# Attention and gated FFN on one core: the last group's reload of gate and input in two lots, and the third kept sum loaded later and added in one run

## Chip, core and metric

The kernel runs on one core of a Trainium2 chip. The metric is the device time of one execution in microseconds (us). One execution was also taken by the hardware profiler; its instructions, waits and transfers are the trace that the text reads.

## What is computed

The reference, cut to what matters (B is the feed-forward branch, A the attention branch):

```python
xn = layernorm(x)                                    # x: 1 x 2048 x 512, bf16
q  = (xn @ wq) as 32 heads of 128                    # keys and values come from a cache of 2048 rows
o  = softmax(q @ k_cache.T * 128**-0.5) @ v_cache    # per head
s  = concat(o) @ wo                                  # 4096 -> 512
h  = relu(xn @ W_gate) * (xn @ W_up)                 # 512 -> 1792
g  = silu(h @ W_down)
return x + s * g
```

## The kernel before

**Blocks and positions.** The attention is 128 blocks (32 heads by four quarters of 512 query rows). A block has eight positions, 0 to 7, one for each pair of 128 keys; the text writes (119, 2) for block 119, position 2. At a position TensorE computes two score tiles (line L1626) three positions ahead, ScalarE takes their exponential into `PT` (L1638), and TensorE multiplies the `PT` of the present position with the values (L1735, 16 products), into the accumulator `ps_acc`. At the end of a block VectorE takes the reciprocal of the sums (L1655) and writes the normalized block to `Onorm` (L1658), of which there are four buffers, used in turn: block b writes buffer b mod 4, and its L1655 waits until the transpose of block b-4 out of that buffer has landed. That transpose is a DMA from SP's queue (`OT_store<-Onorm`, L1663). The values of the next block may go into `ps_acc` once `Onorm` is written.

**Ring of score banks.** The PSUM tile `ps_r` is three slots of two banks. Each pair of score tiles takes the next slot in turn, and so does each side product; a slot is free again when ScalarE or VectorE has read it. TensorE's instructions run in order, so a score tile whose slot isn't free holds all that is behind it.

**Side work.** Eight groups of four heads. While a group runs, the output projection of the group before it is computed by a scheme with seven products in place of eight (as Strassen's), each product's result being added into up to two of four sums `s_acc[:, J, i, :]` (J = 0 to 3, i = 0 to 3). The work is placed by hand: `plan` holds TensorE's products by (block, position), `side` holds calls for the other engines. At a position the score tiles come first, then the items of `plan`, then those of `side`, then the products with the values. The order in which an engine's instructions are issued in the program is the order in which it runs them.

**The last group** is blocks 112 to 127 (`fb` = 112, `LB` = 124). It has, beside the products:

- `load_kept(a)` (L1433), two DMAs that load a kept sum (a = 4, 5, 6; the third is a = 6) from DRAM to the buffers `KR[a]`; `add_kept(a, i)` (L1442) adds its part i on GpSimd into two sums, for a = 6 into J = 1 and J = 3. a = 6 is loaded at (115, 3) and added at (118, 1), (118, 3), (121, 2) and (121, 4) for i = 1, 3, 0, 2.
- `reload_g` at (115, 5): on SP's queue four DMA transposes of the gate from DRAM to `gT` (L1146) and four of the input to `xT` (L1147), alternating, then one plain load of `gN` (L1148).
- `emit_base(0, i)` at (119, 2) to (119, 5): VectorE multiplies a sum by `gT` (L1587; it waits for all four transposes of the gate), GpSimd adds `xT` (L1592; it waits for all four of the input).
- `prep_x(6, 5, part)` (L1488): GpSimd's operand sums for the product j = 5, at (120, 5) and (121, 1); `prep_x(6, 3, part)` for j = 3 at (122, 5) and (123, 1).
- `emit_one(2, 6, 4, 1, 0)` in `plan` at (121, 4): two products (L1457) in one ring slot, whose results VectorE adds (L1388) into J = 1 and J = 3 together, first for i = 1, then for i = 3. Each of the two additions waits for whatever last wrote the sums that it adds to.

On SP's queue the order from block 115 on is: `KT_sb` transpose for head 30 (L366), the reload, the values of head 30 (`V_sb`, L371), the transposes out of `Onorm` of blocks 115, 116, 117 and 118, the keys of head 31, its values, the transpose of block 119, and so on.

Of the kernel before, what the change touches and what calls it, by code (L numbers as in the profile page):

```python
# [30 lines left out]
def _wait(eng, tok):  # L31
    if tok is None:
        return
    sem, val = tok
    if val <= 0:
        return
    eng.wait_ge(sem.h, val)


def _wait_all(eng, toks):  # L40
    best = {}
    for t in toks:
        if t is None:
            continue
        sem, val = t
        k = id(sem)
        if k not in best or best[k][1] < val:
            best[k] = (sem, val)
    for sem, val in best.values():
        _wait(eng, (sem, val))  # L50


def bass_recurrent_scan__mha_block_cached__glu_gated_reglu__prompt_kernel(
# [20 lines left out]
    NT = S // 128  # L74
    DC = D // 128
# [33 lines left out]
    out_t = out2.rearrange("(n p) d -> p n d", p=128)  # L109
# [4 lines left out]
    sp = nc.sync  # L114
    pool = nc.gpsimd

    with ExitStack() as es:
# [9 lines left out]
        def newsem(unit=1):  # L127
            _cnt[0] += 1
            return _Sem(es.enter_context(nc.semaphore(f"sem{_cnt[0]}")), unit)
# [23 lines left out]
        def at_(off, shape, dt, name):  # L153
            _cnt[0] += 1
            return nc.alloc_sbuf_tensor_at(f"{name}_{_cnt[0]}", shape, dt, offset=base[0] + off)
# [68 lines left out]
        gN = at_(104448, [128, 4, D], BF16, "gN")  # L224
# [51 lines left out]
        sem_gn = newsem(16)  # L276
# [597 lines left out]
        def blk_of(gp):  # L874
            b, p = divmod(gp, NP)
            h, Q = divmod(b, QB)
            return b, h, Q, p
# [261 lines left out]
            for Q in range(QB):  # L1139
                sem_gs.sig(sp.dma_start(out_t[:, 4 * Q:4 * Q + 4, :], g_sb[:, 4 * Q:4 * Q + 4, :]))  # L1140

        def reload_g():
            _wait_all(sp, [u_tok["last"], u_tok["add"], sem_gs.cur()])
            for c in range(DC):
                cs = slice(c * 128, (c + 1) * 128)
                sem_gr.sig(sp.dma_start_transpose(gT[:, c, :], out2[:, cs]))  # L1146
                sem_xr.sig(sp.dma_start_transpose(xT[:, c, :], x2[:, cs]))  # L1147
            sem_gn.sig(sp.dma_start(gN[:], out_t[:, NT - 4:NT, :]))  # L1148

        def gu_h(Q, k, gate, up, waits):  # L1150
            _wait_all(pool, waits)
# [259 lines left out]
        one_to = {1: (0, 1), 7: (1, 2), 4: (1, 3)}  # L1411
# [21 lines left out]
                os_tok[("l", a)] = sem_rr[a].sig(sp.dma_start(  # L1433
                    K[n][:].rearrange("p i q -> p (i q)"), swap[a][:, 2 * n * NQ:2 * (n + 1) * NQ]))

        def add_kept(a, i):
            K = KR[a]
            _wait(pool, os_tok[("l", a)])
            for J in one_to[{4: 1, 5: 7, 6: 4}[a]]:
                _wait(pool, os_tok[(J, i)])  # L1440
                d = s_acc[:, J, i, :]
                os_tok[(J, i)] = sem_fo.sig(pool.tensor_tensor(d, d, K[i // 2][:, i % 2, :], ALU.add))  # L1442
# [424 lines left out]
        LB = NBLK - QB  # L1867
        side = {}
# [11 lines left out]
        for g in range(NG - 1):  # L1880
            b0 = (g + 1) * GB
            half = g < NG - 2
# [53 lines left out]
            for k, (j, (r, p)) in enumerate(zip((2, 6, 5, 3), px)):  # L1936
                side.setdefault((b0 + r, p), []).append((prep_x, g, j, 0))
                r, p = max((r, p), (xs[(2, 6, 5)[k - 1]] + 1, 1)) if k else (r, p)
# [28 lines left out]
        for b in range(NBLK):  # L1967
            pr, r = (b - 2) // 8 + 1, (b - 2) % 8
# [13 lines left out]
            elif 0 < pr < NPR:  # L1982
                c, step = r // 4, r % 4
# [9 lines left out]
        for n, (g, j, b) in enumerate(unit_at):  # L1993
# [14 lines left out]
            if j in (5, 7):  # L2008
                side.setdefault((b + 2, 0) if b + 1 in x_at else (b + 1, second[1]), []).append((add_unit, g, j))
        side.setdefault((GB + 1, 0), []).append((spill_g,))  # L2010
        side.setdefault((LB - 9, 5), []).append((reload_g,))
        for g in range(2, NG):
            b = GB * (g - 1)
            side.setdefault((b + 2, 0) if g == 2 else (b + 1, 4), []).append((load_unit_w, g, 0))
            side.setdefault((b + 2, 6) if g == 2 else (b + 2, 3), []).append((scale_unit_w, g, 0))
            b, p = (21, 6) if g == 2 else (b + 3, 5)
            side.setdefault((b, p), []).append((load_unit_w, g, 1))
            b, p = (22, 4) if g == 2 else (b + 1, 3)
# [1 line left out]
            sw = (22, 4) if g == 2 else (GB * (g - 1) + 6, 3)  # L2020
            side.setdefault(sw, []).append((sum_unit_w, g))
        fb = GB * (NG - 1)
        for r, p, a in ((1, 4, 4), (3, 1, 5), (3, 3, 6)):
            side.setdefault((fb + r, p), []).append((load_kept, a))
        for r, p, a, i in ((2, 2, 4, 0), (2, 4, 4, 2), (3, 1, 4, 1), (3, 3, 4, 3), (4, 0, 5, 1), (4, 2, 5, 3), (4, 4, 5, 0),
                           (4, 6, 5, 2), (6, 1, 6, 1), (6, 3, 6, 3), (9, 2, 6, 0), (9, 4, 6, 2)):
            side.setdefault((fb + r, p), []).append((add_kept, a, i))
        for i in range(4):
            side.setdefault((fb + 7, 2 + i), []).append((emit_base, 0, i))
        for i, part, (r, p) in ((1, 0, (11, 1)), (1, 1, (11, 2)), (3, 0, (11, 2)), (3, 1, (11, 3)), (0, 0, (11, 2)), (0, 1, (11, 4)), (2, 0, (11, 4)), (2, 1, (11, 5))):  # L2030
            side.setdefault((fb + r, p), []).append((emit_finish, i, part))
        for k, (J, i) in enumerate(((3, 1), (3, 3), (1, 1), (1, 3))):
            b, p = ((0, 1), (0, 3), (0, 5), (1, 0))[k]
            side.setdefault((LB + b, p), []).append((emit_base, J, i))
            c = 2 * (J // 2) + i // 2
            b, p = ((LB, 6), (LB + 1, 1), (LB + 1, 3), (LB + 1, 5))[k]
            side.setdefault((b, p), []).append((turn_base, c))
        for k, (J, i) in enumerate(((2, 0), (2, 2), (2, 1), (2, 3), (1, 0), (1, 2), (3, 0), (3, 2))):
            b, p = ((1, 2), (1, 3), (1, 4), (2, 4), (2, 3), (2, 5), (3, 1), (3, 3))[k]
# [21 lines left out]
        for gp in range(LAG, TOTP):  # L2061
# [3 lines left out]
            b, h, Q, p = blk_of(gp)  # L2065
# [111 lines left out]
```

## Time and profile before

| | |
|---|---|
| runs of the kernel before | 1236.59, 1237.78, 1238.86 us; median 1237.78 us |
| the profiled execution | 1237.87 us, of which the span of the instructions is 1236.5 us |
| TensorE busy | 1229.6 us of the span |
| ScalarE, VectorE, GpSimd busy | 1042.5, 875.9, 872.8 us |
| granted TensorE clock | 0.999 |

Times inside the profile are counted from the start of the span. In a row of the timeline stand the start, the duration, the engine, the line, the operation, what is written and read with shapes, and how many instructions were merged; in brackets the engine's idle time before it and what ended that. PE is TensorE, PEld its weight loads, DVE VectorE, ACT ScalarE, POOL GpSimd, SPq SP's queue of DMA issues. A row of the waits gives engine, tile and line of the waiter, what it waited for, the total in us, the number of times and the longest.

### The profile page before, as it was taken

The numbers are of one execution on the slowest core, as the hardware profiler recorded it, in microseconds if no ns is written. First come the engines' busy times: TensorE is split into PE (matmuls) and PEld (weight loads), VectorE is DVE, ScalarE is ACT, GpSimd is POOL, SyncE is SP. The second block draws the span as 40 slices with busy tenths as digits, with TensorE's granted clock in tenths as the row PEclk, the third lists the DMA queues.
The fourth block names the chain that finished last, engine by engine and source line by source line (L and its number), as shares of the span: only waits on it lengthen the run. The fifth ranks groups of instructions, "written<-read, shape, count | busy, mean of one in ns | idle before, by whom it ended". The sixth has DMA issues, their size and how long they took to land.

```text
span 1236.5 us, 29347 instructions
## 1 busy us (share of the span) xinstructions
PE 1229.6 (99%) x11922; PEld 816.2 (66%) x11922; DVE 875.9 (71%) x1335; ACT 1042.5 (84%) x1110; POOL 872.8 (71%) x994
## 2 busy tenths in 40 slices
PE   9999999999999999999999999999999999999998
PEld 5466666776666666666666666666666666666665
DVE  7668787667676767677676767676776767575587
ACT  4457877668899998999999999999999999989994
POOL 3355876313767868977978777976888777668668
PEclk9999999999999999999999999999999999999999
DMA  9712331223223534464636664584545464349726
GB/s 276 158 31 37 77 80 24 52 48 97 53 50 54 139 96 120 116 171 101 169 74 151 141 163 87 150 174 102 149 120 132 114 167 95 86 103 183 138 36 141
DMA packets 286646, 137.70 MB, mean 111 GB/s; under 512 B 253872, under 2 KB 279728, under 8 KB 280496
## 3 DMA queue, kind: packets, MB, share of 16 engines
q1 hardware_dynamic: 285168, 135.04, 47.2%
q8 instruction: 95, 1.56, 0.6%
q10 hardware_dynamic: 1344, 0.79, 0.2%
q14 instruction: 39, 0.32, 0.1%
HBM read 63.18 MB, written 30.41 MB: 76 GB/s over the span
## 4 chain that ended last, share of the span: by engine, by line
PE 97%; ACT 2%; DVE 0%; DMA 0%; issue 0%
PE ps_acc L1735 37%; PE ps_r L1626 35%; PE ps_r L1060 5%; PE ps_r L1523 4%; PE ps_r L1177 3%; PE ps_r L1238 3%; ACT PT L1638 2%; PE ps_r L924 2%; PE ps_r L739 2%; PE ps_r L743 2%; PE ps_acc L842 1%; PE ps_r L1457 1%; PE ps_r L1767 1%; PE ps_r L1554 1%; PE ps_r L1555 1%; PE ps_r L1848 0%
## 5 line engine op out<-in xcount | busy, mean ns | idle before, releaser
L1638 ACT ACTIVATE PT<-ps_r 128x1024 bf16<-128x1024 f32 x1024 | 990.7, 1026 | 127.7 <-PE ps_r L1626 112.7
L1735 PEld LDWEIGHTS ps_acc<-V_sb,PT 128*128 128x128 bf16 x8192 | 544.4, 98 | 224.7 <-issue 29.9
L1735 PE MATMUL ps_acc<-V_sb,PT 128*128 128x129 bf16 x8192 | 629.1, 220 | 1.2 <-ACT PT L1638 1.2
L1626 PE MATMUL ps_r<-QT_sb,KT_sb 128*128 128x512 bf16 x2048 | 601.0, 379 | 0.4
L1065 DVE TENSOR_TENSOR UVR<-UVR,ps_r 128x512 f32<-128x512 f32 (+1 forms) x228 | 168.7, 755 | 79.0 <-PE ps_r L1060 76.6
L1626 PEld LDWEIGHTS ps_r<-QT_sb,KT_sb 128*128 128x128 bf16 x2048 | 163.8, 98 | 31.2 <-ACT PT L1638 1.5
L1388 DVE TENSOR_TENSOR s_acc<-s_acc,ps_r 128x1024 f32<-128x1024 f32 x97 | 117.8, 1219 | 30.6 <-PE ps_r L1555 16.9
L1404 DVE TENSOR_TENSOR s_acc<-s_acc,ps_r 128x512 f32<-128x512 f32 x170 | 113.4, 685 | 27.7 <-PE ps_r L1523 21.9
L1655 DVE RECIPROCAL rz_sb<-ps_acc 128x4 f32<-128x4 f32 x127 | 23.2, 182 | 100.7 <-PE ps_acc L1735 97.0
L1488 POOL TENSOR_TENSOR TI<-OT_store 128x512 f16<-128x512 bf16 (+1 forms) x48 | 54.7, 1161 | 53.9 <-issue 22.2
L1658 DVE TENSOR_TENSOR Onorm<-ps_acc,rz_sb 128x512 bf16<-128x512 f32 x127 | 87.8, 691 | 4.4
L1488 POOL TENSOR_TENSOR TI<-OX 128x512 f16<-128x512 f16 x38 | 43.1, 1155 | 64.4 <-issue 62.8
L1065 DVE TENSOR_TENSOR QT_sb<-UVR,ps_r 128x512 bf16<-128x512 f32 x72 | 49.5, 687 | 34.3 <-PE ps_r L1060 31.9
L1025 POOL TENSOR_TENSOR TI<-xn_sb 128x512 f16<-128x512 f16 x48 | 55.8, 1163 | 18.4 <-PE ps_r L1060 18.4
L1332 POOL TENSOR_TENSOR WX<-Wo_sb 128x512 f16<-128x512 bf16 x7 | 8.1, 1156 | 68.5 <-DVE dbuf L1247 39.0
L1025 POOL TENSOR_TENSOR TI<-xn_sb,TI 128x512 f16<-128x512 f16 x48 | 55.9, 1164 | 0.0
L1523 PE MATMUL ps_r<-TI,SI 128*128 128x512 f16 x129 | 48.9, 379 | 0.0
L1060 PE MATMUL ps_r<-TI,SI 128*128 128x512 f16 x126 | 47.9, 380 | 0.0
L1025 POOL TENSOR_TENSOR TI<-xnT 128x512 f16<-128x512 bf16 x36 | 41.6, 1156 | 4.5 <-PE ps_r L1060 4.5
L1153 POOL TENSOR_SCALAR gB<-gB 128x512 bf16<-128x512 bf16 x14 | 20.8, 1485 | 30.4 <-DVE gB L1183 30.4
L1025 POOL TENSOR_TENSOR TI<-xnT,TI 128x512 f16<-128x512 bf16 x36 | 41.6, 1155 | 0.0
L1133 POOL TENSOR_TENSOR QT_sb<-UVR,UVR 128x512 bf16<-128x512 f32 x24 | 29.8, 1272 | 6.7 <-DVE UVR L1065 6.7
(236 smaller groups left out, 1461.6 us busy)
## 6 DMA issues: line engine op xcount, KB each, us to landing
sums<-s_acc SPq DMA_DIRECT2D x25, 1024.0 KB, 4.4
s_acc<-sums SPq DMA_DIRECT2D x22, 1024.0 KB, 5.7
V_sb<-in_A_v_cache_dram SPq DMA_DIRECT2D x32, 512.0 KB, 4.6
Wq_sb<-in_A_wq_dram SPq DMA_DIRECT2D x16, 256.0 KB, 3.5
Wo_sb<-in_A_wo_dram SPq DMA_DIRECT2D x8, 512.0 KB, 4.2
KR<-sums SPq DMA_DIRECT2D x6, 512.0 KB, 4.8
out_dram<-g_sb SPq DMA_DIRECT2D x4, 512.0 KB, 4.5
OT_store<-Onorm SPq DMA_TRANSPOSE x127, 2.8
```

The costliest lines, as they stand in the source:

```text
L1025: return sem_ui.sig(pool.tensor_tensor(dst, x, y, o))
L1060: return sem_up.sig(pe.matmul(dst, lhs, rhs, start=start, stop=stop, skip_group_check=True))
L1065: dve.tensor_tensor(dst, x, ps, ALU.add))
L1177: ins = pe.matmul(ps_r[:, bank, :], L(i), R(i), start=(i == 0), stop=(i == HC - 1))
L1388: t = sem_opa.sig(dve.tensor_tensor(dst, dst, sb, op))
L1404: t = dve.tensor_tensor(dst, dst, sb, op)
L1488: return sem_oi.sig(pool.tensor_tensor(dst, x, y, o))
L1523: return sem_op.sig(pe.matmul(dst, lhs, rhs, start=start, stop=stop, skip_group_check=True))
L1626: ins = pe.matmul(ps_r[:, 2 * s + tt, :], KT_sb[h % 2][:, t * 128:(t + 1) * 128], QT_sb[qt_slot[(h, Q)]][:], start=True, stop=True)
L1638: act.activation(PT[pb][:], ps_r[:, 2 * s:2 * s + 2, :], ACTF.Exp, scale=scale / WSC)
L1658: dve.tensor_tensor(Onorm[ob][:], o_ap, rz_sb[:].to_broadcast([128, 4, Dh]), ALU.mult))
L1735: ins = pe.matmul(o_ap, PT[pb][:, tt, j * 128:(j + 1) * 128], V_sb[vb][:, t, 0:VW], start=(t == 0 and j % 2 == 0), stop=(t == KT - 1 and j ...
```

## The change

```diff
-        def reload_g():
+        def reload_g(half):
             _wait_all(sp, [u_tok["last"], u_tok["add"], sem_gs.cur()])
-            for c in range(DC):
+            for c in range(DC // 2 * half, DC // 2 * (half + 1)):
                 cs = slice(c * 128, (c + 1) * 128)
                 sem_gr.sig(sp.dma_start_transpose(gT[:, c, :], out2[:, cs]))
                 sem_xr.sig(sp.dma_start_transpose(xT[:, c, :], x2[:, cs]))
-            sem_gn.sig(sp.dma_start(gN[:], out_t[:, NT - 4:NT, :]))
+            if half:
+                sem_gn.sig(sp.dma_start(gN[:], out_t[:, NT - 4:NT, :]))
...
-        def add_kept(a, i):
+        def add_kept(a, i, js=None):
             K = KR[a]
             _wait(pool, os_tok[("l", a)])
-            for J in one_to[{4: 1, 5: 7, 6: 4}[a]]:
+            for J in js or one_to[{4: 1, 5: 7, 6: 4}[a]]:
                 _wait(pool, os_tok[(J, i)])
...
-        side.setdefault((LB - 9, 5), []).append((reload_g,))
+        side.setdefault((LB - 9, 5), []).append((reload_g, 0))
+        side.setdefault((LB - 7, 1), []).append((reload_g, 1))
...
-        for r, p, a in ((1, 4, 4), (3, 1, 5), (3, 3, 6)):
+        for r, p, a in ((1, 4, 4), (3, 1, 5), (7, 4, 6)):
             side.setdefault((fb + r, p), []).append((load_kept, a))
         for r, p, a, i in ((2, 2, 4, 0), (2, 4, 4, 2), (3, 1, 4, 1), (3, 3, 4, 3), (4, 0, 5, 1), (4, 2, 5, 3), (4, 4, 5, 0),
-                           (4, 6, 5, 2), (6, 1, 6, 1), (6, 3, 6, 3), (9, 2, 6, 0), (9, 4, 6, 2)):
+                           (4, 6, 5, 2)):
             side.setdefault((fb + r, p), []).append((add_kept, a, i))
+        for k in range(8):
+            side.setdefault((fb + 9, 2 + k // 2), []).append((add_kept, 6, k % 4, (1,) if k > 3 else (3,)))
```

In blocks and positions: the reload's first two pairs of transposes stay at (115, 5); the other two pairs and the load of `gN` go to (117, 1), which on SP's queue is behind the values of head 30 and the transposes out of `Onorm` of blocks 115 and 116, and ahead of that of block 117. The load of the third kept sum goes from (115, 3) to (119, 4), behind the transpose of block 118 and ahead of the keys of head 31. Its eight additions (four parts into two sums) all stand in block 121: into J = 3 for i = 0 and 1 at position 2, for i = 2 and 3 at position 3, then into J = 1 for i = 0 and 1 at position 4, for i = 2 and 3 at position 5. The products of `plan` at (121, 4) are issued between those at position 3 and those at position 4.

## Prediction

> **What bounds the kernel now.** I read the page first, then the waits by engine, then the timeline of blocks 115 to 122, where every edit lies. The page's engine line and its chain:
>
> ```profile
> PE 1229.6 (99%) x11922; PEld 816.2 (66%) x11922; DVE 875.9 (71%) x1335; ACT 1042.5 (84%) x1110; POOL 872.8 (71%) x994
> PE 97%; ACT 2%; DVE 0%; DMA 0%; issue 0%
> ```
>
> TensorE has work all through and 97% of the chain that ends last is its own. The change takes no matmul away, so it can gain only where TensorE stands still. TensorE's waits over the whole trace, then the stretches before, in and after the one wait in this region (span, then busy time by engine):
>
> ```profile
> PE ps_acc L1735 <- ACT PT L1638: 1.2, 1, 1.2
> ...
> 1085.00:1155.00 70.00, 70.00 (x735) 48.29 (x733) 44.27 (x57) 65.56 (x70) 52.90 (x51) 1.00 0.76 160
> 1155.30:1157.60 2.30, 1.13 (x5) 0.19 (x3) 0.98 (x3) 2.30 (x3) 1.21 (x2) 1.00 0.57 96
> 1157.60:1226.00 68.40, 68.36 (x684) 45.82 (x685) 55.14 (x75) 55.78 (x60) 49.79 (x45) 1.00 0.42 71
> ```
>
> There is one stall, between blocks 119 and 120, and beside it no idle time that could be won or that could swallow a new delay. The timeline shows its size. Last products of block 119 and first of block 120, then the same border between blocks 121 and 122:
>
> ```profile
> 1154.39 0.62 PE L1735 MATMUL ps_acc<-V_sb,PT 128*128 128x129 bf16 x8
> 1157.64 0.27 PE L1735 MATMUL ps_acc<-V_sb,PT 128*128 128x129 bf16 x2 [1.21 <-ACT PT L1638]
> ...
> 1172.49 0.62 PE L1735 MATMUL ps_acc<-V_sb,PT 128*128 128x129 bf16 x8
> 1174.28 0.84 PE L1735 MATMUL ps_acc<-V_sb,PT 128*128 128x129 bf16 x12
> ```
>
> In both, four score tiles and two side products lie between. From start to start it is 3.25 us at the first border and 1.79 us at the second, so the stall costs 1.46 us. The row names ScalarE, but what block 120 needs is block 119's normalization, and VectorE's rows say who held that:
>
> ```profile
> 1147.37 0.18 DVE L1655 RECIPROCAL rz_sb<-ps_acc 128x4 f32<-128x4 f32 x1 [4.73 <-PE ps_acc L1735]
> 1148.83 1.22 DVE L1388 TENSOR_TENSOR s_acc<-s_acc,ps_r 128x1024 f32<-128x1024 f32 x1 [0.55 <-PE ps_r L1457]
> 1149.96 4.41 DVE L1587 SCALAR_TENSOR_TENSOR s_acc<-s_acc,gT 128x512 f32<-128x512 f32 x4
> 1156.59 0.18 DVE L1655 RECIPROCAL rz_sb<-ps_acc 128x4 f32<-128x4 f32 x1 [2.21 <-DMA OT_store<-Onorm]
> 1156.80 0.69 DVE L1658 TENSOR_TENSOR Onorm<-ps_acc,rz_sb 128x512 bf16<-128x512 f32 x1
> ```
>
> VectorE waited 2.21 us for the transpose that empties the buffer of block 115. `Onorm` is written at 1157.49 and TensorE goes on at 1157.64. SP's queue shows why that transpose was late (the landing of each follows in the next fence):
>
> ```profile
> 1086.82 3.01 SPq L366 DMA_TRANSPOSE KT_sb<-in_A_k_cache_dram  x1
> ...
> 1120.16 6.67 SPq L366 DMA_TRANSPOSE KT_sb<-in_A_k_cache_dram  x1
> 1126.95 2.78 SPq L1146 DMA_TRANSPOSE gT<-out_dram  x1
> ...
> 1134.97 2.68 SPq L1147 DMA_TRANSPOSE xT<-in_A_x_dram  x1
> 1137.69 3.08 SPq L1146 DMA_TRANSPOSE gT<-out_dram  x1
> ...
> 1143.20 2.51 SPq L1146 DMA_TRANSPOSE gT<-out_dram  x1
> ...
> 1148.81 0.51 SPq L371 DMA_DIRECT2D V_sb<-in_A_v_cache_dram  x1
> 1149.36 5.24 SPq L1663 DMA_TRANSPOSE OT_store<-Onorm  x1
> 1154.64 3.88 SPq L1663 DMA_TRANSPOSE OT_store<-Onorm  x3
> ```
>
> The landings, from the view of DMA issues over a window around one issue each (the 1149.36 one; the last gate transpose; the later half of the third kept sum), and VectorE's row that wrote block 115's buffer:
>
> ```profile
> OT_store<-Onorm SPq DMA_TRANSPOSE x1, 7.1
> ...
> gT<-out_dram SPq DMA_TRANSPOSE x1, 5.2
> ...
> KR<-sums SPq DMA_DIRECT2D x1, 512.0 KB, 7.2
> ...
> 1123.90 0.69 DVE L1658 TENSOR_TENSOR Onorm<-ps_acc,rz_sb 128x512 bf16<-128x512 f32 x1
> ```
>
> Block 115 was normalized at 1124.6, but its transpose stood behind the whole reload: issued at 1149.36, blocked for 5.24 us at issue, landed 7.1 us after its start, at 1156.5.
>
> **The reload in two lots: −1.46 us.** In the changed order the transposes of blocks 115 and 116 stand behind four transposes, not eight. Four take 1126.95 to 1137.65 to issue; even with the block of 5.24 us and the 7.1 us to landing, block 115's buffer is empty by 1138.2 + 7.1 = 1145.3, 9 us ahead of when it is wanted (about 1154.9: the last products start at 1154.39, and in the row of 1147.37 and its like VectorE follows by 0.5). Block 116's buffer is wanted one block later. The values of head 30 come earlier too. So the old stall goes whole; bounds 1.21 (the idle time in TensorE's row) to 1.46, and I take the latter, which counts the loss and not only the part shown as idle.
>
> What is late next there is the last gate transpose, since `emit_base` in block 119 waits for all four. Before, it landed at 1143.20 + 5.2 = 1148.4, and VectorE wanted it at 1149.96. Now it has in front of it the values (0.51 us of issue) and two `Onorm` transposes (the first 1.3 us, a third of the row of 3.88, to 5.24 us; the second 1.3), but not the load of the third kept sum, which moves behind. That load is 1 MB that stood in front of the keys: their issue took 6.67 us behind it and 3.01 us without, so the first lot starts 3.7 us sooner. Net, the landing moves by 0.5 + 1.3 + 1.3 − 3.7 = −0.6 us to 0.5 + 5.2 + 1.3 − 3.7 = +3.3 us: 1147.8 to 1151.7. The queue before the first `Onorm` transpose is shorter than in the old trace (four transposes and the values, where it was eight, `gN` and the values), so I take the middle, about 1150, which is a wait of nearly nothing. The four multiplications then end near 1154.4 and the reciprocal is wanted at 1154.9. GpSimd's additions behind them are 5.71 us long and its next job, the operand sums for j = 5, starts 4.3 us after they end:
>
> ```profile
> 1150.79 5.71 POOL L1592 TENSOR_TENSOR s_acc<-s_acc,xT 128x512 f32<-128x512 f32 x4 [3.78 <-DVE s_acc L1587]
> 1160.81 2.27 POOL L1488 TENSOR_TENSOR TI<-OT_store 128x512 f16<-128x512 f16 x2 [4.30 <-issue]
> ```
>
> so the input's landing may slip by 4 us unseen. The load of the third kept sum, issued near 1156, lands within the 7.2 us that it took before, by 1163, and GpSimd wants it near 1167: nothing. The keys and values of head 31 move behind it by the same 3.7 us and are wanted in block 124, three blocks on: nothing.
>
> **The additions in one run: +2.80 us.** The count of additions is unchanged (eight); four leave block 118, where nobody waited for them. In block 121 they are new company for `emit_one` at (121, 4). Before, the part i = 0 was added ahead of it and it touches i = 1 and i = 3, so VectorE didn't wait for GpSimd. Now the four additions into J = 3 stand ahead, and VectorE's first addition needs the second of them, its second the fourth. Rows of GpSimd (the last is the operand sums for j = 3), VectorE and TensorE in blocks 121 and 122:
>
> ```profile
> 1168.14 1.71 POOL L1442 TENSOR_TENSOR s_acc<-s_acc,KR 128x512 f32<-128x512 f32 x1
> 1169.81 1.27 POOL L1442 TENSOR_TENSOR s_acc<-s_acc,KR 128x512 f32<-128x512 f32 x1
> 1171.05 1.27 POOL L1442 TENSOR_TENSOR s_acc<-s_acc,KR 128x512 f32<-128x512 f32 x1
> 1172.28 1.26 POOL L1442 TENSOR_TENSOR s_acc<-s_acc,KR 128x512 f32<-128x512 f32 x1
> 1177.45 2.26 POOL L1488 TENSOR_TENSOR TI<-OX 128x512 f16<-128x512 f16 x2 [3.90 <-issue]
> ...
> 1167.81 0.91 DVE L1359 TENSOR_TENSOR OX<-OX,OT_store 128x1024 f16<-128x1024 f16 x1
> 1169.61 2.35 DVE L1388 TENSOR_TENSOR s_acc<-s_acc,ps_r 128x1024 f32<-128x1024 f32 x2 [0.89 <-PE ps_r L1457]
> ...
> 1172.06 0.59 PE L1626 MATMUL ps_r<-QT_sb,KT_sb 128*128 128x512 bf16 x2
> ```
>
> The run starts behind the same operand sums, which wait for TensorE, so it keeps its place against TensorE and I work on the old clock. Four additions end at 1172.28 + 1.26 = 1173.54. VectorE's second addition starts then, not at 1170.8, takes 1.22 (row of 1148.83) and ends at 1174.76, where it ended at 1169.61 + 2.35 = 1171.96: 2.80 us later. Who waits: the ring has three slots, the two products of `emit_one` hold one until both additions are done, and the third pair of score tiles after it takes that slot. That is the pair of 1172.06, which begins 0.1 us after the old end, so it now begins near 1174.86, and behind it in TensorE's order stand the last products of block 121, and behind those on VectorE the reciprocal. All of block 121's end moves by 2.80. ScalarE has at most two pairs in hand then and runs dry; TensorE is busy 68.36 of the next 68.40 us, so nothing is caught up. Bounds: 2.35 if the first addition takes 1.27 like the others and not 1.71; 4.1 if all four take 1.71. I take 2.80, the rows of this very place.
>
> Why the first takes 1.71: VectorE was in an fp16 operation with two SBUF operands until 1168.72. The Trainium skill (SBUF — State Buffer, "Who interferes with whom") says that such an operation and a GpSimd instruction that reads SBUF shut each other out for a whole instruction, while one with a single SBUF input doesn't. By that rule the additions beside VectorE's L1388 (one operand in PSUM) keep 1.27, and the rows agree; the sum would stay 2.80.
>
> Behind it: the additions into J = 1 follow until 1178.5 on the old clock, and the operand sums for j = 3 wait for TensorE, which is then at 1177.45 + 2.80 = 1180.3, so they aren't delayed. J = 1 is next read in block 123.
>
> **Sum.** 2.80 − 1.46 = +1.34 us. On the profiled execution's 1237.87 (1.4 us of it outside the span, unchanged) that is 1239.2; it lies 0.09 above the median, so against the median 1237.78 I predict 1239.1.
>
> **Rivals.** (1) *Gain only*: VectorE's additions don't reach TensorE, because the slot or the order is not as I read it. For it: block 121's side work has slack everywhere else. Against it: the score tiles of 1172.06 begin 0.1 us after the additions' old end. Then 1237.8 − 1.5 = 1236.3, faster by 0.12%; it decides if the fourth addition ends before 1170.7. To pass 0.2% it would need a second gain that I don't see. (2) *The second lot comes late*: the gate lands after about 1150.7, the multiplications push the reciprocal of block 119, and a new wait stands where the old one stood. At the bound of 1151.7 they end at 1156.1, 1.2 after the wish. The reciprocal and L1658 take 0.9 us and TensorE without the old stall would go on at 1157.64 − 1.46 = 1156.18, so some 0.2 of that is slack: +1.0. If the keys' issue gains nothing from the moved load, the landing is 3.7 later, at 1155.4: +4.7. Halfway, +2.8 on my 1239.1 is 1241.9; slower. For it: the queue is full from the keys to the last lot. Against it: the moved load, and that input landing late too would leave VectorE alone. Its first multiplication, before GpSimd began, was short, the third, beside GpSimd, long (rows below), so four undisturbed ones would take 2.7 us and not 4.41:
>
> ```profile
> 1149.96 0.68 DVE L1587 SCALAR_TENSOR_TENSOR s_acc<-s_acc,gT 128x512 f32<-128x512 f32 x1
> 1151.17 1.65 DVE L1587 SCALAR_TENSOR_TENSOR s_acc<-s_acc,gT 128x512 f32<-128x512 f32 x1
> ```
>
> (3) *The old wait stays*, since the `Onorm` transpose is still late: +2.8, 1240.6; against it stand 9 us of margin.
>
> **How the numbers follow.** My forecast 0.54, rival 1 0.12, rival 2 0.28 (the queue's order is certain, its speed is not), rival 3 0.06. The three runs lie within 1.2 us of their median, and 0.2% (2.5 us) is about what a measurement of this kernel can tell from no change. My case is inside it but for its upper part (4.1 − 1.2 = +2.9 at the bounds; 0.12 of the 0.54); rival 1 leaves 0.05 of its chance beyond the bound of faster; of rival 2 0.27 and rival 3's 0.06 are over. So faster 0.05, same 0.50, slower 0.45. The range leaves out the far half of rival 2 and takes in the end of rival 1 that lies nearer to no change: 1236.8 to 1242.0. My case alone is 1238.7 (2.35 − 1.46) to 1240.7 (4.1 − 1.2).
>
> **What would show it.** Right: L1655 of block 119 without a wait for the DMA; L1146 in two pairs with two L1663 between; in block 121 L1388 waiting for GpSimd's L1442 twice, its second ending at the fourth addition plus 1.2; a gap of 2.8 us in TensorE before the last products of that block. Wrong: no such gap; L1587 waiting for `gT` and the reciprocal of block 119 behind it; the first `Onorm` transpose landing after 1154.

## The result and the profile after

Against 1238.44 us before (median of 12 runs), the changed kernel took 1241.8 us (median of 12). The ratio is 1.0024, 95% interval 1.0015 to 1.0033: slower by 0.24%, 3.0 us (the medians differ by 3.4). (Ratios here are against runs of the kernel before on the same chip; beside experiments 1 to 4 its median was 1238.55 us, beside 5 and 6 1238.47, and the ratios of experiments 1 to 4 lie 0.0003 to 0.0005 under the quotients of the medians.) The profiled execution has a span of 1240.4 us. Lines from `reload_g` on are one or two higher than before: score tiles L1627, values L1736, VectorE's additions L1389, GpSimd's L1443, reciprocal L1656.

The first sight is TensorE's list of waits. Before, the longest was 1.2 us, at the border between blocks 119 and 120. The two longest now:

```profile
PE ps_r L1627 <- DVE s_acc L1389: 3.1, 1, 3.1
PE ps_r L485 <- PEq L2166: 0.8, 1, 0.8
```

The old wait is gone, and another of 3.1 us is there: score tiles that wait for VectorE's additions. VectorE's timeline in blocks 119 and 121 shows both:

```profile
1150.15 4.42 DVE L1588 SCALAR_TENSOR_TENSOR s_acc<-s_acc,gT 128x512 f32<-128x512 f32 x4
1155.23 0.18 DVE L1656 RECIPROCAL rz_sb<-ps_acc 128x4 f32<-128x4 f32 x1 [0.66 <-PE ps_acc L1736]
...
1163.52 0.18 DVE L1656 RECIPROCAL rz_sb<-ps_acc 128x4 f32<-128x4 f32 x1 [2.70 <-PE ps_acc L1736]
...
1170.02 1.22 DVE L1389 TENSOR_TENSOR s_acc<-s_acc,ps_r 128x1024 f32<-128x1024 f32 x1 [2.48 <-POOL s_acc L1443]
1172.47 1.22 DVE L1389 TENSOR_TENSOR s_acc<-s_acc,ps_r 128x1024 f32<-128x1024 f32 x1 [1.23 <-POOL s_acc L1443]
1175.69 0.18 DVE L1656 RECIPROCAL rz_sb<-ps_acc 128x4 f32<-128x4 f32 x1 [2.00 <-PE ps_acc L1736]
```

The reciprocal of block 119 (1155.23) now waits for TensorE and not for a transpose. In block 121 VectorE waits twice for GpSimd, where before it began at 1169.61 and made both additions without a break. GpSimd's first four additions:

```profile
1166.95 1.71 POOL L1443 TENSOR_TENSOR s_acc<-s_acc,KR 128x512 f32<-128x512 f32 x1
1168.63 1.26 POOL L1443 TENSOR_TENSOR s_acc<-s_acc,KR 128x512 f32<-128x512 f32 x1
1169.86 1.27 POOL L1443 TENSOR_TENSOR s_acc<-s_acc,KR 128x512 f32<-128x512 f32 x1
1171.09 1.25 POOL L1443 TENSOR_TENSOR s_acc<-s_acc,KR 128x512 f32<-128x512 f32 x1
```

The second ends at 1169.89 and VectorE starts at 1170.02; the fourth ends at 1172.34 and VectorE starts its second at 1172.47, which ends at 1173.69. What TensorE does then is the one thing that the prediction did not have. Its timeline, and the busy time with the granted clock in three stretches (the clock is the third number from the end):

```profile
1170.42 0.62 PE L1736 MATMUL ps_acc<-V_sb,PT 128*128 128x129 bf16 x8
1174.15 0.63 PE L1627 MATMUL ps_r<-QT_sb,KT_sb 128*128 128x512 bf16 x1 [3.11 <-DVE s_acc L1389]
1174.57 1.07 PE L1736 MATMUL ps_acc<-V_sb,PT 128*128 128x129 bf16 x8
1175.44 1.77 PE L1627 MATMUL ps_r<-QT_sb,KT_sb 128*128 128x512 bf16 x4
1177.05 0.38 PE L1524 MATMUL ps_r<-OT_store,WX 128*128 128x512 f16 x1
```

```profile
1171.00:1173.50 2.50, 0.04 (x1) 0.00 (x0) 1.27 (x2) 0.68 (x1) 2.50 (x3) 1.00 0.00 0
1173.60:1176.90 3.30, 2.75 (x13) 1.75 (x15) 0.97 (x3) 1.39 (x2) 3.30 (x3) 0.50 0.00 0
1177.00:1180.00 3.00, 3.00 (x33) 2.06 (x32) 1.97 (x3) 2.46 (x3) 0.23 (x1) 1.00 0.58 52
```

The last product before the stop ends at 1171.04 (1170.42 + 0.62). The row of 1174.15 has one of the two score tiles; the weights of the first are loaded from 1173.74 on, so its record is missing and the stop lasted about 2.7 us and not 3.1:

```profile
1173.74 0.13 PEld L1627 LDWEIGHTS ps_r<-QT_sb,KT_sb 128*128 128x128 bf16 x2 [2.88 <-DVE s_acc L1389]
```

About 2.5 us after that last product the granted clock falls to one half, and it stays there until about 1176.9, some 3.4 us. Eight products with the values take 1.07 us (0.62 just before the stop), four score tiles 1.77 us (1.03 before the change). So the stop is paid twice, once as waiting and once as slow work.

How much each block lost can be read from the reciprocals. From that of block 118 to that of block 120 it was 1164.70 − 1147.37 = 17.33 us (the row of 1164.70 is in the next fence, with that of block 122) and is 1163.52 − 1147.56 = 15.96: −1.37. From block 120 to block 122 it was 1181.34 − 1164.70 = 16.64 and is 1184.55 − 1163.52 = 21.03: +4.39. The sum is +3.02, the 3.0 us of the measured ratio. Rows of the kernel before:

```profile
1164.70 0.18 DVE L1655 RECIPROCAL rz_sb<-ps_acc 128x4 f32<-128x4 f32 x1 [2.70 <-PE ps_acc L1735]
1181.34 0.18 DVE L1655 RECIPROCAL rz_sb<-ps_acc 128x4 f32<-128x4 f32 x1 [2.70 <-PE ps_acc L1735]
```

and of the changed kernel:

```profile
1147.56 0.18 DVE L1656 RECIPROCAL rz_sb<-ps_acc 128x4 f32<-128x4 f32 x1 [4.73 <-PE ps_acc L1736]
1184.55 0.18 DVE L1656 RECIPROCAL rz_sb<-ps_acc 128x4 f32<-128x4 f32 x1 [2.70 <-PE ps_acc L1736]
```

These two differences, A over the first border and B over the second, are the yardstick for the experiments. The profiled spans differ by 3.9 us; 0.2 of the rest lies ahead of block 119 and 0.7 behind the reciprocal of block 122, nearly all of it at the last stores: from the last reciprocal of four columns to the end it took 20.9 to 22.0 us in the profiles of this study, 21.7 in both the fastest and the slowest kernel.

### The profile page after: what moved, and what is told of

Read it like the earlier page. It is cut to its first block, busy times and chain, and to the rows that moved or that the text cites. A ratio compares the mean times of both kernels' runs of the same rounds, so it can differ in the third digit from the quotient of the medians.

```text
span 1240.4 us, 29144 instructions
## 1 busy us (share of the span) xinstructions
PE 1219.7 (98%) x11712; PEld 817.2 (66%) x11922; DVE 876.2 (71%) x1335; ACT 1042.8 (84%) x1110; POOL 874.2 (70%) x994
## 4 chain that ended last, share of the span: by engine, by line
PE 96%; ACT 2%; issue 1%; POOL 1%; DVE 1%; DMA 0%; DVEq 0%; POOLq 0%
PE ps_acc L1736 37%; PE ps_r L1627 34%; PE ps_r L1060 5%; PE ps_r L1524 4%; PE ps_r L1178 3%; PE ps_r L1239 3%; PE ps_r L924 2%; ACT PT L1639 2%; PE ps_r L739 2%; PE ps_r L743 2%; PE ps_acc L842 1%; PE ps_r L1768 1%; PE ps_r L1458 1%; PE ps_r L1556 1%; PE ps_r L1555 1%
## 5 line engine op out<-in xcount | busy, mean ns | idle before, releaser
L1736 PEld LDWEIGHTS ps_acc<-V_sb,PT 128*128 128x128 bf16 x8192 | 544.9, 98 | 223.6 <-issue 28.5
L1736 PE MATMUL ps_acc<-V_sb,PT 128*128 128x129 bf16 x8192 | 629.6, 220 | 1.0
L1627 PE MATMUL ps_r<-QT_sb,KT_sb 128*128 128x512 bf16 x1849 | 555.9, 380 | 13.1 <-DVE s_acc L1389 3.1
L1627 PEld LDWEIGHTS ps_r<-QT_sb,KT_sb 128*128 128x128 bf16 x2048 | 164.0, 98 | 34.4 <-DVE s_acc L1389 2.9
L1389 DVE TENSOR_TENSOR s_acc<-s_acc,ps_r 128x1024 f32<-128x1024 f32 x97 | 117.9, 1219 | 33.4 <-PE ps_r L1556 16.9
L1656 DVE RECIPROCAL rz_sb<-ps_acc 128x4 f32<-128x4 f32 x127 | 23.2, 183 | 100.0 <-PE ps_acc L1736 98.5
```

Of the source, the lines that this page charges most:

```text
L1389: t = sem_opa.sig(dve.tensor_tensor(dst, dst, sb, op))
L1627: ins = pe.matmul(ps_r[:, 2 * s + tt, :], KT_sb[h % 2][:, t * 128:(t + 1) * 128], QT_sb[qt_slot[(h, Q)]][:], start=True, stop=True)
L1736: ins = pe.matmul(o_ap, PT[pb][:, tt, j * 128:(j + 1) * 128], V_sb[vb][:, t, 0:VW], start=(t == 0 and j % 2 == 0), stop=(t == KT - 1 and j ...
```

## The experiments

My theory after the result: the whole loss is the wait for the second and fourth addition plus the half clock after that stop; the gain at block 119 comes from the queue. Rivals: it is the run's place or length; the slow matmuls come of something else than the stop; the gain comes from the split alone.

**1. The same run in another order.** The eight additions stand where the change put them, but those for i = 0 and 2 (both sums) come ahead of the two products and those for i = 3 and 1 behind:

```diff
-        for k in range(8):
-            ... (add_kept, 6, k % 4, (1,) if k > 3 else (3,))
+        for k, (J, i) in enumerate(((3, 0), (3, 2), (1, 0), (1, 2), (3, 3), (3, 1), (1, 3), (1, 1))):
+            ... (add_kept, 6, i, (J,))
```

> The changed kernel with the eight additions in another order: i = 0 and 2 into J = 3 and J = 1 ahead of the two products at (121, 4), i = 3 and 1 behind them. My theory (the whole loss is VectorE waiting for the second and fourth addition, TensorE behind it, and the half clock after that stop): no wait of L1389 for L1443, no gap in TensorE in block 121, granted clock 1.00 there; 4.6 us less than the changed kernel, 1.5 us less than the kernel before (ratio about 0.9988). Rival (the loss is the run's place or length, or the moved load, whatever the order): block 121 still ends late, ratio above 1.001.

Measured: 1237.39 us, ratio 0.9986 (0.9977 to 0.9995): faster than both kernels. VectorE's two additions in its timeline:

```profile
1168.65 2.35 DVE L1389 TENSOR_TENSOR s_acc<-s_acc,ps_r 128x1024 f32<-128x1024 f32 x2 [0.89 <-PE ps_r L1458]
1172.19 0.18 DVE L1656 RECIPROCAL rz_sb<-ps_acc 128x4 f32<-128x4 f32 x1 [1.19 <-PE ps_acc L1736]
```

They wait for TensorE's product and not for GpSimd, as before the change. A is −1.37, B 0.00 (16.64 us). The run's length and place cost nothing; its order was the whole loss.

**2. One addition less to wait for.**

```diff
-        for k in range(8):
-            ... (add_kept, 6, k % 4, (1,) if k > 3 else (3,))
+        for k, (J, i) in enumerate(((3, 0), (3, 1), (3, 3), (3, 2), (1, 0), (1, 1), (1, 2), (1, 3))):
+            ... (add_kept, 6, i, (J,))
```

> The changed kernel with (J = 3, i = 3) as third of the eight additions and not as fourth, so that VectorE's second addition waits for one addition less. The gap of TensorE before the score tiles of block 121's last position shrinks by one addition, 1.23 us, from 3.0 to 1.8 us. If the half clock needs a stop of about 3 us, the clock stays at 1.00 and the loss falls by 1.23 + 1.5 = 2.7 us, to 1.8 (0.3 us above the kernel before, ratio 1.0003). If the half clock comes with any such stop, the loss falls by 1.2 only (1.9 us above before, ratio 1.0015).

Measured: 1239.14 us, ratio 1.0002 (0.9993 to 1.0011). B is +1.63. TensorE's timeline, and its clock behind the stop:

```profile
1172.53 0.60 PE L1627 MATMUL ps_r<-QT_sb,KT_sb 128*128 128x512 bf16 x2 [1.50 <-DVE s_acc L1389]
1172.97 0.62 PE L1736 MATMUL ps_acc<-V_sb,PT 128*128 128x129 bf16 x8
1173.43 1.03 PE L1627 MATMUL ps_r<-QT_sb,KT_sb 128*128 128x512 bf16 x4
```

```profile
1171.00:1174.00 3.00, 1.50 (x14) 0.96 (x14) 1.80 (x4) 1.50 (x2) 3.00 (x4) 1.00 0.00 0
1174.00:1177.00 3.00, 3.00 (x34) 2.01 (x32) 2.34 (x4) 2.77 (x4) 3.00 (x3) 1.00 0.55 49
```

One addition of 1.25 us less in the wait took 2.76 us off the loss (4.39 − 1.63): this shorter stop left the clock alone, and the other runs of this kernel had a mean granted clock of 0.999 or more too. That is the first of the two alternatives in the expectation.

**3. The same wait with TensorE kept busy.** The changed kernel with

```diff
+            if (bq, pq) == (GB * (NG - 1) + 9, 7):
+                for _i in range(44):
+                    pe.matmul(ps_acc[:, 0, 132:252], ident[:], ident[:, 0:120], start=False, stop=False, ...)
```

ahead of the score tiles that wait.

> The changed kernel with 44 extra matmuls of 120 columns ahead of the score tiles that wait in block 121, into columns of the accumulator that nobody reads: about 2.5 us of work on TensorE inside its stop of 3.0 us. Theory (1.5 us of the loss is the half clock after an idle TensorE): the clock stays at 1.00 behind the wait, the score tiles start at the same time, and the kernel is 1.5 us faster than the changed one although it does more; some 1.6 us above the kernel before (ratio 1.0013). Rival (the slow matmuls behind the wait come of something else, such as empty weight or score buffers): the clock still shows 0.50 and the time is that of the changed kernel (ratio 1.0024).

Measured: 1238.98 us, ratio 1.0000 (0.9991 to 1.0009).

```profile
1170.82 2.47 PE L2080 MATMUL ps_acc<-ident 128*128 128x120 bf16 x44
1173.70 0.60 PE L1627 MATMUL ps_r<-QT_sb,KT_sb 128*128 128x512 bf16 x2 [0.40 <-DVE s_acc L1389]
1174.14 0.62 PE L1736 MATMUL ps_acc<-V_sb,PT 128*128 128x129 bf16 x8
1174.59 1.03 PE L1627 MATMUL ps_r<-QT_sb,KT_sb 128*128 128x512 bf16 x4
```

VectorE still waits 2.5 and 1.2 us for GpSimd, and the score tiles start when they may, but they run at full clock (four of them in 1.03 us): B is +2.84, not +4.39. Forty-four useless matmuls took 1.55 us off. So in the traces the wait by itself is 2.84 us and the half clock 1.55 us. (The measured times are better than that. A and B together are +1.47 us against the kernel before, or 1.0012, where the interval ends at 1.0009 and the medians differ by 0.4 us; against the changed kernel the median is 2.8 us less. Of the 2.4 us between the two profiled spans, 1240.4 and 1238.0, 0.8 lies at the last stores; why the rest of the times don't fit isn't known.)

**4. The change without the split.** The reload stays whole at (115, 5); load and additions are as changed:

```diff
-        side.setdefault((LB - 7, 1), []).append((reload_g, 1))
+        side.setdefault((LB - 9, 5), []).append((reload_g, 1))
```

> The changed kernel with the reload in one lot at (115, 5) as before; load and additions of the third kept sum as changed. If the old stall went by the split alone, the reciprocal of block 119 waits for the Onorm transpose as before (about 2 us) and the time is 1.5 us above the changed kernel. If the moved load is enough (1 MB less ahead of the keys, 3.6 us; the transpose of block 115 lands near 1152.9 where it is wanted at 1154.9), there is no wait for it and the time equals that of the changed kernel (ratio 1.0024). I expect the latter.

Measured: 1241.19 us, ratio 1.0017 (1.0008 to 1.0026). A is −1.37 as with the split, B +4.52 with the same half clock. SP's rows show how (the keys of head 30, and the first transpose out of `Onorm` behind the reload):

```profile
1120.05 3.49 SPq L366 DMA_TRANSPOSE KT_sb<-in_A_k_cache_dram  x1
...
1146.24 5.06 SPq L1664 DMA_TRANSPOSE OT_store<-Onorm  x1
```

Without the load ahead of them the keys take 3.49 us to issue and not 6.67, and all behind them comes 3 us sooner: the transpose of block 115 starts at 1146.24 and not at 1149.36, enough for a wait of 2.21 us. The old stall went by the moved load; the split wasn't needed for it.

**5. The split alone.** Reload split, load and additions as in the kernel before.

> The kernel before with the reload split as in the change; load and additions of the third kept sum stay where they were. The transpose of block 115 stands behind four transposes and lands before 1146: no wait of the reciprocal of block 119 for it. But the 1 MB of the third kept sum is still ahead of the keys, so the second lot is some 3.5 us later than in the changed kernel and the last gate transpose lands near 1151.7, where VectorE wants it at 1150.0. Theory: VectorE waits some 1.7 us for gT, then does its four multiplications in 2.5 us since the input is late too, and ends before the reciprocal is due at 1154.9: 1.5 us less than the kernel before (ratio 0.9988). Rival (the multiplications take 4.4 us as before): they end at 1156.1, TensorE stops for about 1 us between blocks 119 and 120, 0.5 us less than before (ratio 0.9996). In both block 121 is as before.

Measured: 1239.04 us, ratio 1.0005 (0.9994 to 1.0016). A is +0.50, B 0.00.

```profile
1153.69 3.46 DVE L1588 SCALAR_TENSOR_TENSOR s_acc<-s_acc,gT 128x512 f32<-128x512 f32 x4 [3.68 <-DMA gT<-out_dram]
1157.07 0.17 DVE L1656 RECIPROCAL rz_sb<-ps_acc 128x4 f32<-128x4 f32 x1
```

No wait for the transpose any more, but one of 3.68 us for the gate's second lot, and the reciprocal right behind the multiplications, 0.5 us later than before. Both theories had the landing 2 us too early (1151.7 for 1153.6). This is the prediction's second rival, in the kernel in which the load still stands ahead.

**6. The load moved, the run in the harmless order, no split** (experiments 1 and 4 together).

> The reload in one lot as before, the load of the third kept sum at (119, 4), the eight additions in block 121 in the order that the two products don't wait for. If the moved load alone takes the old stall away, no wait for the Onorm transpose in block 119, none for GpSimd in block 121, and the time of the kernel with the split and this order (ratio 0.9986 there). If the split is needed as well, a stop of about 1.5 us between blocks 119 and 120 and the time of the kernel before (ratio 1.000).

Measured: 1237.42 us, ratio 0.9992 (0.9983 to 1.0000); A −1.37, B 0.00, as in experiment 1, and the medians are alike (1237.39 and 1237.42). The interval touches 1, so as a verdict of its own it is thin; with the whole reload the first transpose has about 1 us to spare, with the split over 10.

## Why the prediction was right or wrong

The direction and the places were right; the time lay inside the range, above my likeliest case (1238.7 to 1240.7).

That the time lay inside the range is luck. My own case, counted as a difference, ended at 4.1 − 1.2 = +2.9, and its upper end of 1240.7 lies 1.1 us below what was measured; the range reached 1242.0 for the sake of the second rival, which did not happen. And 0.7 us of the 1241.8 is a base higher than the one I counted from (1238.44 against 1237.78).

*The old stall goes: −1.46 forecast, −1.37 measured.* Right, but credited to the wrong edit. The step "block 115's buffer is empty by 1145.3" holds: in the changed kernel that transpose was issued at 1134.47, and the view of DMA issues gives 5.3 us to landing as the median of the two. SP's rows for it and for the last gate transpose:

```profile
1134.47 3.72 SPq L1664 DMA_TRANSPOSE OT_store<-Onorm  x2
...
1143.15 2.32 SPq L1146 DMA_TRANSPOSE gT<-out_dram  x1
```

But the split wasn't needed for it: experiment 4 has no split and the same gain. I used the 3.7 us of the moved load only to bring the gate in time and never asked what they do alone.

*The second lot in time.* Right: VectorE began its multiplications at 1150.15 without a wait. The last gate transpose landed 5.0 us after its issue, at 1148.2, nearer to the early end of my 1147.8 to 1151.7 than to "about 1150"; with the same queue in experiment 2 VectorE waited 0.68 us for it, until 1150.90. Experiment 5 shows that it hung on the moved load.

*VectorE waits for the second and fourth addition, the ring holds the score tiles: +2.80 forecast.* The chain is as described, step for step, and the wait by itself is +2.84 (experiment 3). The rows that I summed were the right ones, even to the 1.71 us of the first addition, which came in again beside VectorE's fp16 operation (in the changed kernel the third addition ran beside VectorE's first, of 1170.02, and took 1.27; the second, with VectorE idle, took 1.26).

*What was missed: +1.55 us of half clock.* The step that failed is "all of block 121's end moves by 2.80", with "nothing is caught up" as the only thought of what follows a stop. The term should have been 2.84 + 1.55 = 4.39. In the trace of before the one stop in the body, of 1.2 us, left the clock at 1.00, and the prediction says nothing of the clock. The end of that trace showed a fall. Its last matmuls in TensorE's timeline, and the two stretches behind them:

```profile
1231.81 0.40 PE L1795 MATMUL ps_r<-ident,gT 128*128 128x128 bf16 x4
```

```profile
1232.20:1234.10 1.90, 0.00 (x1) 0.00 (x0) 1.11 (x2) 0.59 (x1) 1.13 (x2) 1.00 0.83 242
1234.20:1236.40 2.20, 0.00 (x0) 0.00 (x0) 0.00 (x0) 0.00 (x0) 0.00 (x0) 0.50 0.79 251
```

The last matmul ends at 1232.2 and the clock is at one half from 1234.1 on: a fall 1.9 us after it, so a stop forecast at 2.8 us was long enough to be hit. The Trainium skill warns of such a fall (TensorE: Matmul & The Clock Gate, "Why this matters for your kernels": no idle gaps over about 3 us, or the clock falls back to half). The measured falls came sooner than that figure says: in the profiled executions the stops of the kernel before and of experiments 2 and 5 (1.2, 1.5 and 1.7 us in the lists of waits) left the clock at 1.00, and those of the changed kernel and of experiment 4, both about 2.7 us, halved it.

*The sum:* 4.39 − 1.37 = +3.0, where I had 2.80 − 1.46 = +1.34. My bound for the wait, 4.1, came near the 4.39 for a wrong reason: it stood for slower additions, and these took what I had said.

*Rivals.* "Gain only" fell, but is what experiments 1 and 6 make of the change. "The second lot comes late" didn't happen in it. "The old wait stays" fell.

## What to carry to other kernels

When additions commute, their order still is a chain: put those that the next product's result doesn't touch ahead of it, and the rest behind; here that alone was 4.4 us. Price a new wait on the engine that sets the pace by its length and by what the clock may do after it. And when a change has several edits on one queue, ask of each what it does alone: one moved load did what the split was there for.

## What the runs showed of the hardware that was not expected

A stop of TensorE can cost in steps: 1.25 us less waiting (experiment 2) saved 2.76 us, since the clock no longer fell. Filling 2.47 us of the wait with matmuls that nobody reads kept the clock at 1.00 and saved 1.55 us. The half clock lasted 3.4 us in the changed kernel and in experiment 4.

The length of a stop alone does not decide when the clock falls. It fell about 2.5 us after the last product in the changed kernel and 1.9 us after the last matmul in the kernel before. In experiment 3's kernel the last matmuls end at 1233.88, and the clock stayed whole for 4.5 us more:

```profile
1233.48 0.40 PE L1796 MATMUL ps_r<-ident,gT 128*128 128x128 bf16 x4
```

```profile
1233.90:1238.40 4.50, 0.00 (x0) 0.00 (x0) 1.09 (x2) 0.59 (x1) 1.11 (x1) 1.00 0.76 233
1238.50:1238.90 0.40, 0.00 (x0) 0.00 (x0) 0.00 (x0) 0.00 (x0) 0.00 (x0) 0.50 0.00 0
```

The moments of the changes say more. The clock of the changed kernel in three short stretches, then that of experiment 4:

```profile
1173.50:1173.60 0.10, 0.00 (x0) 0.00 (x0) 0.10 (x1) 0.00 (x0) 0.10 (x2) 0.66 0.00 0
1176.90:1177.00 0.10, 0.10 (x2) 0.00 (x0) 0.00 (x0) 0.10 (x1) 0.10 (x1) 0.78 0.00 0
1238.30:1238.40 0.10, 0.00 (x0) 0.00 (x0) 0.00 (x0) 0.00 (x0) 0.00 (x0) 0.93 1.05 359
...
1173.70:1173.80 0.10, 0.10 (x1) 0.08 (x2) 0.00 (x0) 0.00 (x0) 0.10 (x1) 0.73 0.00 0
1177.10:1177.20 0.10, 0.10 (x2) 0.09 (x1) 0.00 (x0) 0.10 (x1) 0.05 (x1) 0.70 0.00 0
1238.55:1238.65 0.10, 0.00 (x0) 0.00 (x0) 0.00 (x0) 0.00 (x0) 0.00 (x0) 0.75 0.92 272
```

A mean between 0.50 and 1.00 gives the moment: 0.66 is full clock for a third of the stretch, so a fall at 1173.53. The clock rises at 1176.94 and falls again, behind the last matmul, at 1238.39. In experiment 4 the moments are 1173.75, 1177.16 and 1238.60. In both traces the rise comes 3.41 us after the fall and the last fall 64.85 us after the first, which is 19 times 3.413. That fits a gate that looks at fixed moments, which a stop meets early or late, as the Trainium skill has it (TensorE: Matmul & The Clock Gate, "What's actually happening": a free-running window of some 3.4 us).

Counted back in such steps from the fall at the end of each trace, it is the idle time up to a moment that matters. It was 2.49 us in the changed kernel's stop and 1.91 us at the end of the kernel before, and the clock fell. In experiment 3's kernel the last fall is at 1238.49, and one step earlier TensorE had been idle for 1.19 us only; in experiment 2's the last fall is at 1235.04, and the stop of 1.5 us (1171.04 to 1172.53) lies whole between the moments 1170.18 and 1173.60, 19 and 18 steps earlier. Neither made the clock fall. So the limit lies between 1.5 and 1.9 us here. That is an estimate from these four places: no run moved a stop of one length against the moments.

The mean clocks of single runs suggest that the same kernel can meet both cases. Of experiment 4's ten runs, five had a mean granted clock of 0.998 and took 1241.6 us or more, five had 0.999 and took 1240.8 us or less. Of experiment 5's eleven runs three, and of the 54 runs of the kernel before beside the experiments seven, were at 0.998 or lower and took at least 1240.4 us; of the 43 runs of experiments 1, 2, 3 and 6 none was. Where those runs lost the clock isn't shown, so a half clock priced from one trace is the price of that execution.

Four multiplications of VectorE beside GpSimd's additions took 4.42 us in the changed kernel. They took 2.50 us in experiment 2, where the input came late and GpSimd's additions began at 1154.40, after them (the wait for the gate, 0.68 us, hurt nobody):

```profile
1150.90 2.50 DVE L1588 SCALAR_TENSOR_TENSOR s_acc<-s_acc,gT 128x512 f32<-128x512 f32 x4 [0.68 <-DMA gT<-out_dram]
1155.23 0.18 DVE L1656 RECIPROCAL rz_sb<-ps_acc 128x4 f32<-128x4 f32 x1 [1.83 <-PE ps_acc L1736]
```
